# Reordering the head and the ticks of a DeltaNet and expert kernel

## The chip, the cores and the metric

The kernel runs on one core of a Trainium2 chip, as one program. The metric is the device time of one execution in microseconds. Its engines work on their own queues and in order: TensorE (PE, with its weight loads listed apart as PEld), VectorE (DVE), ScalarE (ACT), GpSimd (POOL) and SyncE (SP, which here only issues DMAs).

## The reference, cut to what matters

```
q, k, v: (4 batches, 8 heads, 768 positions, 48), beta: (4, 8, 768), float32
k_n = k / (norm(k) + 1e-6);  state = 0                      # state: 48 x 48 for each batch and head
for t in range(768):
    y[t]  = q[t] @ state
    state = state + beta[t] * outer(k_n[t], v[t] - k_n[t] @ state)
x = y of all heads side by side                             # 3072 tokens x 384
logits = x @ w_gate;  e = argmax(logits);  gate = softmax(logits)[e]
out = gate * (relu(x @ w1[e]) @ w2[e])                      # 8 experts, 384 -> 1024 -> 384
```

The recurrence is over positions. It is computed in blocks of 128 positions: with the products K K^T of a block known, the effect of the positions on each other is a triangular system, whose inverse turns residuals (v less what the state gives for k) into the updates u. Then y = q state + masked(Q K^T) u, and the state grows by K^T u.

## The kernel before, in words

There are NT = 6 blocks of 128 positions, B = 4 batches, so NN = 24 pieces n = 4 tb + b (block tb, batch b). Each block is split into four quarters of 32 positions. The order of all instructions is written out by hand (manual_schedule): a generator stands for a chain of work, and each `run` emits one step of it. Every engine executes what it is given in that order, so an instruction that waits holds up all that is behind it on its engine.

**Head.** Keys of the first four pieces are loaded, the diagonal 32 x 32 blocks of K K^T are made for block 0 (`kpart`, first step, "db") and inverse 0 runs on VectorE: `prepare(0)`, then `lanes(0)`, a forward substitution on 32 rows for 4 quarters and 32 batch-head pairs at once, in 32 steps of products (L332) and differences (L343) and 19 of the combination (L353, L361), then the turn into `wt` (L376). Beside it the other keys, v and q are loaded on SP, each load held back until a step of the inverse is done (`load`, `tiles["hold"]`). TensorE makes the full K K^T of eight pieces in the order `FILL` (`halves`, two PSUM banks of the pool "g", both evicted by ScalarE, L234); for blocks after 0 the diagonal blocks go to DRAM (`gd`, L239) and come back turned (`lg`, L243). Then come `dummy(W0)`, matmuls of 512 columns into a bank "x" with no use of their result, and `scale_v(0)`.

**Ticks.** The main loop has 27 ticks (t from 0 to 26). In tick t the first quarter of piece t, the second of t - 1, the third of t - 2 and the fourth of t - 3 are treated together, each on its 32 partitions. A tick emits, in this order:

- `residual(t)`: what state and earlier updates give for the keys, in PSUM "ks" (PE L403, L415); VectorE subtracts it from v (L422)
- `beside(t, 0)`: side work, see below
- `chunk(qs_, t)`: Q K^T of a piece (`qpart`, PE L252), eviction (ACT L262), mask on GpSimd (L263)
- `scale_v(t + 1)`: v times the key's norm (DVE L385); `clear_u`: a zero fill on GpSimd
- `beside(t, 1)`, then `dummy(WD.get(t, 0))`
- `apply(t)`: inverse times residual (PE L430), copied to u (ACT L434)
- `run(fin)`: the last part of the piece that was begun a tick earlier, x's turn (`emit_x`: PE L497, row copy ACT L498, reduction of the gate logits DVE L499); every so many pieces it starts `emit_slots` (a generator in `fine`), which finds each token's slot and scatters the rows (POOL L580)
- `beside(t, 2)`, and then the new `finish(t - 3)` in three steps: q times state (PE L449), state update (PE L459, ACT L463), masked Q K^T times u and y's copies (PE L469, ACT L473), with `beside` between them
- `chunk(ks_, t)`: K K^T of a later piece, `beside(t, 6)`, a zero fill of a DRAM region

`beside(t, i)` emits `STEPS[i]` steps (`STEPS0[i]` for t < 8) of the current inverse (`inverses`), up to three more of its `prepare`, `FINE[i]` steps of `emit_slots`, and at late ticks weight pieces and early expert work. Block tb's inverse has to be done before tick 4 tb; what is left then is emitted ahead of that tick.

**Slots.** `emit_slots` makes its counts on TensorE (L537, L540) into free columns of the bank "x" of the latest `emit_x`, and VectorE reads them (L544, L546 updates `base`).

**Expert phase.** From tick 20 on weights are loaded and split into high and low parts, and expert 0 begins; after tick 26 come the eight experts.

Of the kernel before, what the change touches and what calls it, by code (L numbers as in the profile page):

```python
# [42 lines left out]
def deltanet_moe(ctx, tc, qT, kT, kr, v, beta, w_gate, w1, w2, out):  # L43
# [62 lines left out]
    LAG = NB - 1  # L106
    FILL = (4, 5, 6, 0, 7, 1, 2, 3)

    STEPS = (3, 2, 3, 2, 2, 2, 2)

    STEPS0 = (3, 3, 3, 2, 2, 2, 2)
    FINE = (3, 3, 3, 2, 2, 2, 2)
    W0 = 18
    WD = {0: 10, 1: 6, 2: 6, 4: 6, 8: 6, 12: 6, 16: 6, 20: 6}
    W1 = 4
# [50 lines left out]
    tiles = {tb: {b: {} for b in range(B)} for tb in range(NT)}  # L166

    def load(out, in_):
        ins = nc.sync.dma_start(out=out, in_=in_)
        if "hold" in tiles:  # L170
            tc.add_manual_dep(ins.ins, tiles["hold"].name,
                              mybir.DependencyInfo(mybir.DependencyClass.Sync, mybir.DependencyReason.DATA),
                              reason="later loads wait")

# [34 lines left out]
    def kpart(n):  # L209
# [4 lines left out]
        if tb == 0:  # L214
# [16 lines left out]
            yield  # L231
        pg = halves(f"pg{tb}_{b}", kt, kt)
        for a in range(2):
# [11 lines left out]

    def halves(nm, kt, xt):

        pg = [psg_[-1].tile([128, NP, C], F32, name=f"{nm}_{a}", tag="g") for a in range(2)]
        for p in range(NP):
            for a in range(2):  # L250
                r = slice(64 * a, 64 * a + D)
                nc.tensor.matmul(pg[a][:, p], lhsT=kt[r, p], rhs=xt[r, p], start=True, stop=True,  # L252
                                 tile_position=(64 * a, 0), skip_group_check=True)
        return pg

    def qpart(n):

        tb, b = n // B, n % B
        pm = pm_t[n % QSL]
        pg = halves(f"pq{tb}_{b}", kt_t[n % KTL], qt_t[n % QTL])  # L260
        for a in range(2):
            nc.scalar.copy(out=pm[:, a:H:2], in_=pg[a])  # L262
        nc.gpsimd.affine_select(out=pm, in_=pm, compare_op=ALU.is_gt, fill=0.0, base=0,  # L263
                                pattern=[[0, H], [1, C]], channel_multiplier=-1)
        yield

    def clear_w(tb):
# [10 lines left out]
    def prepare(tb):  # L278
# [29 lines left out]
        yield  # L308
        def norms():
            for q in range(NB):  # L310
                p = slice(32 * q, 32 * q + 32)
                nc.vector.transpose(out=nt_t[p, (B * tb + q) * H:(B * tb + q) * H + 32], in_=s0[p])
                yield

# [7 lines left out]
    def lanes(tb):  # L322
# [23 lines left out]
        def combine(g):  # L346
# [11 lines left out]
            while n > 1:  # L358
                h, k = n // 2, n - n // 2
                y = x[:, :, 0:h] if n > 2 else lw[:, r0:r0 + 4, 0:HB].unsqueeze(2)  # L360
                nc.vector.tensor_tensor(out=y, in0=x[:, :, 0:h], in1=x[:, :, k:n], op=ALU.add)  # L361
                n = k
                yield
# [10 lines left out]
        yield  # L374
        T["wt"] = lp.tile([128, BH, 32], F32, name=f"wt{tb}", tag="wt", bufs=2)
        nc.vector.transpose(out=T["wt"].rearrange("p h t -> p t h"), in_=lw)  # L376
        if tb + 2 < NT:
# [46 lines left out]
    def apply(t):  # L424

        ks, vn = tiles["ks", t], vt[t]
        for h in range(H):
            for q, n in stage(t):
                r = slice(32 * q, 32 * q + 32)
                nc.tensor.matmul(ks[r, h, :], lhsT=tiles[n // B]["wt"][r, n % B * H + h, :], rhs=vn[r, h, :],  # L430
                                 start=True, stop=True, tile_position=(32 * q, 32 * q), skip_group_check=True)
# [6 lines left out]
    def finish(n):  # L438
# [41 lines left out]
        if j % m == 0:  # L480
            pool, tag = (fp, "rowb") if j >= 2 else (rp, "row") if n < NN - 2 else (xq_[0], "row")
            t = pool.tile([128, 2 if n < NN - 2 else 1, ROW], F32, name=f"row{tb}_{b}", tag=tag, bufs=2)
            tiles["rows"].append(t[:, 0:m])
        emit_x(n, yt, tiles["rows"][-1][:, j % m], tiles["rl"][:, j])
        if j == w - 1:
# [5 lines left out]

    def emit_x(n, yt, row, rl):

# [4 lines left out]
        nc.scalar.copy(out=row[:, 0:DM].rearrange("t (p c) -> t p c", p=NP), in_=xp[:, :, 0:2 * D])  # L498
        nc.vector.tensor_reduce(out=rl, in_=xp[:, :, 2 * D:].rearrange("t p e -> t e p"), axis=AX.X, op=ALU.add)  # L499

# [103 lines left out]
    def dummy(k):  # L604

        if k:
            wm = pss.tile([128, 512], F32, name=f"wm{next(cnt)}", tag="x")
        for _ in range(k):
# [221 lines left out]
    def more(n=1):  # L830
        for f, x in loads[:n]:
            tiles["hold"] = tiles["mark"]
            f(*((0, x) if f is load_v else (x,)))
# [68 lines left out]
    for t in range(NN + LAG):  # L902
        if t < NN and t % B == 0 and t > 0:
            while queue and queue[0][0] <= t // B:
                inverses(1, t)
            if t == NN - B:
# [3 lines left out]
                W = pieces()  # L910
                run(W)
        residual(t)
        if LAG <= t < NN - KTL + LAG:
            load_kt(t - LAG + KTL)
        beside(t, 0)
        chunk(qs_, t)
        if t + 1 < NN + LAG:
            scale_v(t + 1)
# [5 lines left out]
        run(copies, 2)  # L924
        run(fin)
        for tb in range(1, NT):
            for i in range(NB):
                if t == B * (tb - 1) + i:
                    load_v(tb, i)
        beside(t, 2)  # L930
        fin = finish(t - LAG) if t >= LAG else iter(())
        run(fin)
        beside(t, 3)
        run(fin)
        beside(t, 4)
# [288 lines left out]
```

## Time and profile before

| | |
|---|---|
| median of 3 runs | 578.01 us (576.63 to 578.91) |
| profiled execution | 578.77 us, its span 577.1 us |
| mean granted TensorE clock | 0.949 |
| PE busy | 507.3 us (88%) |
| DVE busy | 352.7 us (61%) |
| ACT busy | 254.8 us (44%) |
| POOL busy | 112.8 us (20%) |

The span begins at the first and ends at the last instruction; all times in the rows below count from its start. In the windows, the number of instructions stands behind each busy time, and the last two columns are the DMA engines' mean busy share and GB/s. Residual t begins at 42.20 us for t = 0, 75.06 for t = 4, 246.64 for t = 20 and 314.27 for t = 26. [...] A busy share is an average over stages that differ in what bounds them.

### The profile page before, as it was taken

The page shows a single profiled execution, that of the slowest core. Times are in us where ns is not written, and L with a number is a line of the kernel's source. Part 1 is how long each engine was busy: PE and PEld are TensorE (multiplying, and loading weights), DVE is VectorE, ACT ScalarE, POOL GpSimd, SP SyncE. Part 2 cuts the span into 40 slices and gives each one's busy share as a digit, 9 for nine tenths or more (in the row PEclk, how much of TensorE's full clock was granted, in tenths as well). Part 3 has the DMA queues.
Part 4 walks back from the last instruction along what each step waited for, and adds up shares of the span by engine and source line. Part 5 has one row for each costly group of instructions (what it writes and reads, how often), then busy time and mean ns, then how long its engine had stood idle before and what let it go on. Part 6 is the DMA issues. An engine that isn't in the chain of part 4 may idle for free.

```text
span 577.1 us, 17370 instructions
## 1 busy us (share of the span) xinstructions
PE 507.3 (88%) x7282; PEld 447.3 (78%) x7282; DVE 352.7 (61%) x1041; ACT 254.8 (44%) x536; POOL 112.8 (20%) x146
## 2 busy tenths in 40 slices
PE   3899599888878958788889899999999999999992
PEld 2767478767757836676678789999999999999992
DVE  2958959848858959844634229656475655655310
ACT  2323356545535724546634225445453635354310
POOL 5010212114113214313122111030203021211111
PEclk9999999879779979889989979999999999999997
DMA  3871576726615526264631254847474647563000
GB/s 108 242 195 38 165 225 181 186 92 171 182 43 194 134 61 198 92 204 153 206 106 44 71 118 156 191 153 182 133 161 143 171 145 163 154 150 98 26 17 24
DMA packets 77053, 79.00 MB, mean 137 GB/s; under 512 B 45721, under 2 KB 64714, under 8 KB 76972
## 3 DMA queue, kind: packets, MB, share of 16 engines
q1 hardware_dynamic: 73516, 68.29, 43.6%
q0 software_dynamic: 3456, 9.57, 4.5%
q8 instruction: 58, 0.95, 0.7%
q14 instruction: 23, 0.19, 0.1%
HBM read 54.25 MB, written 24.37 MB: 136 GB/s over the span
## 4 chain that ended last, share of the span: by engine, by line
PE 47%; DVE 8%; ACT 3%; issue 2%; DMA 2%; POOL 1%; SPq 0%; ACTq 0%; POOLq 0%; DVEq 0%
PE h L726 19%; PE y L736 16%; PE y L1018 4%; PE xp L497 1%; PE ks L430 1%; PE yp L469 1%; ACT u L434 1%; DVE lw L343 1%; DMA xr<-xg 1%; PE ks L403 1%; PE pq L252 1%; PE wm L609 1%; DVE ta L332 1%; ACT row L498 1%; PE ks L415 1%
## 5 line engine op out<-in xcount | busy, mean ns | idle before, releaser
L736 PE MATMUL y<-w2h,hx 128*128 128x384 f32 x352 | 92.8, 338 | 0.1
L739 POOL DMA_INDIRECT out_dram<-yo,idx x32 | 39.4, 1231 | 204.2 <-ACT yo L1013 116.7
L434 ACT COPY u<-ks 32x384 f32<-32x384 f32 x96 | 45.1, 469 | 51.9 <-PE ks L430 47.5
L736 PEld LDWEIGHTS y<-w2h,hx 128*128 128x128 f32 x352 | 64.0, 188 | 0.8 <-DVE hx L730 0.7
L726 PE MATMUL h<-xh,w1l 128*128 128x448 f32 x168 | 61.3, 365 | 0.0
L726 PE MATMUL h<-xl,w1h 128*128 128x448 f32 x168 | 61.2, 364 | 0.0
L726 PE MATMUL h<-xh,w1h 128*128 128x448 f32 x168 | 61.0, 363 | 0.0
L736 PE MATMUL y<-w2l,hx 128*128 128x384 f32 x176 | 59.3, 337 | 0.0
L730 DVE SCALAR_TENSOR_TENSOR hx<-h,hx 128x448 fp32r<-128x448 f32 (+1 forms) x64 | 37.6, 587 | 31.6 <-ACT hx L729 30.9
L616 DVE TENSOR_TENSOR w2l<-w2r,w2h 128x768 fp32r<-128x768 f32 x32 | 30.5, 957 | 42.3 <-ACT w2h L615 41.8
L729 ACT ACTIVATE hx<-h 128x448 fp32r<-128x448 f32 (+1 forms) x64 | 33.2, 519 | 49.6 <-PE h L726 46.2
L263 POOL TENSOR_SCALAR_AFFINE_SELECT pm<-pm 128x1024 f32<-128x1024 f32 x24 | 28.0, 1165 | 132.8 <-ACT pm L262 126.3
L403 PE MATMUL ks<-st,kt 112*32 112x96 f32 x768 | 45.9, 253 | 3.5 <-issue 3.0
L252 PE MATMUL pg<-kt 48*128 48x128 f32 x384 | 40.5, 342 | 8.3 <-DMA kt<-in_kT_dram 4.9
L262 ACT COPY pm<-pq 128x512 f32<-128x512 f32 x48 | 25.7, 588 | 45.8 <-PE pq L252 45.8
L252 PEld LDWEIGHTS pg<-kt 48*128 48x128 f32 x384 | 34.4, 236 | 14.1 <-issue 6.9
L430 PEld LDWEIGHTS ks<-v_all,wt 32*32 32x32 f32 x1536 | 22.1, 112 | 26.6 <-DVE v_all L422 20.6
L430 PE MATMUL ks<-v_all,wt 32*32 32x48 f32 x1536 | 26.0, 212 | 18.6 <-DVE v_all L422 18.0
L1013 ACT ACTIVATE yo<-y,gt 128x384 f32<-128x384 f32 x22 | 12.8, 581 | 63.7 <-PE y L736 36.3
L403 PEld LDWEIGHTS ks<-st,kt 112*32 112x32 f32 x768 | 33.6, 112 | 9.3 <-issue 5.0
L609 PE MATMUL wm<-zrow 128*128 128x512 bf16 x86 | 27.6, 476 | 14.9 <-DVE base L546 13.5
L499 DVE TENSOR_REDUCE rl<-xp 128x8 f32<-128x32 f32 x24 | 4.6, 191 | 53.7 <-ACT row L498 53.7
(161 smaller groups left out, 1103.5 us busy)
## 6 DMA issues: line engine op xcount, KB each, us to landing
w1r<-in_w_dram SPq DMA_DIRECT2D x24, 512.0 KB
w2r<-in_w_dram SPq DMA_DIRECT2D x32, 384.0 KB
xg<-zrow SPq DMA_DIRECT2D x7, 788.0 KB
kt<-in_kT_dram SPq DMA_DIRECT2D x24, 224.0 KB
qt<-in_qT_dram SPq DMA_DIRECT2D x24, 224.0 KB
xr<-xg SPq DMA_DIRECT2D x28, 168.0 KB
xn<-row SPq DMA_DIRECT2D x10, 394.0 KB
ku<-in_kr_dram SPq DMA_DIRECT2D x20, 192.0 KB
```

The source lines that it names most:

```text
L252: nc.tensor.matmul(pg[a][:, p], lhsT=kt[r, p], rhs=xt[r, p], start=True, stop=True, tile_position=(64 * a, 0), skip_group_check=True)
L263: nc.gpsimd.affine_select(out=pm, in_=pm, compare_op=ALU.is_gt, fill=0.0, base=0, pattern=[[0, H], [1, C]], channel_multiplier=-1)
L403: nc.tensor.matmul(ks[32 * q:32 * q + 32, 2 * p:2 * p + 2, :], lhsT=kt_t[n % KTL][0:RP, p, 32 * q:32 * q + 32], rhs=st_view(n % B, p), sta ...
L430: nc.tensor.matmul(ks[r, h, :], lhsT=tiles[n // B]["wt"][r, n % B * H + h, :], rhs=vn[r, h, :], start=True, stop=True, tile_position=(32 * ...
L434: nc.scalar.copy(out=uview(n)[r], in_=ks[r])
L609: nc.tensor.matmul(wm, lhsT=busy[:, 0:128], rhs=busy, start=True, stop=True)
L616: nc.vector.tensor_tensor(out=lo, in0=src, in1=hi.bitcast(F32), op=ALU.subtract)
L726: nc.tensor.matmul(ps, lhsT=w[:, d, fs], rhs=x_[:, d], start=(n == 0), stop=(n == len(terms) - 1))
L729: nc.scalar.activation(out=hh, in_=ps, func=AF.Relu)
L730: nc.vector.scalar_tensor_tensor(out=hl, in0=ps, scalar=0.0, in1=hh.bitcast(F32), op0=ALU.max, op1=ALU.subtract)
L736: nc.tensor.matmul(ps, lhsT=h(f)[h_], rhs=w2[w][:, f, :], start=(n == 0), stop=(n == len(terms) - 1))
L739: nc.gpsimd.indirect_dma_start(out=out, out_offset=bass.IndirectOffsetOnAxis(ap=idx, axis=0), in_=yo, in_offset=None, bounds_check=N - 1, ...
```

## The change

In the head: the order `FILL`, every second K K^T in the y banks, fewer dummies, written to a bank of y. In the ticks: x's turn of the earlier piece right after the residual and its reduction after `beside(t, 0)`; Q K^T after the first step of `finish`; the mask emitted just before the next residual, with a wait for the last step of the inverse before it (`after`, `tiles["mark"]`); 20 or 21 steps of the inverse in a tick; dummies in ticks 0 to 3 alone; v scaled four ticks at a time; v loaded one tick earlier. In the inverse: one transpose of the norms and four DMAs in place of four transposes, and a turn whose output is contiguous (`wt` is read with a step).

```diff
-    FILL = (4, 5, 6, 0, 7, 1, 2, 3)
-    STEPS = (3, 2, 3, 2, 2, 2, 2)
-    STEPS0 = (3, 3, 3, 2, 2, 2, 2)
+    FILL = (0, 1, 4, 5, 6, 7, 2, 3)
+    STEPS = (3, 3, 3, 3, 3, 3, 2)
+    STEPS0 = (3, 3, 3, 3, 3, 3, 3)
-    W0 = 18
-    WD = {0: 10, 1: 6, 2: 6, 4: 6, 8: 6, 12: 6, 16: 6, 20: 6}
+    W0 = 14
+    WD = {0: 6, 1: 6, 2: 6, 3: 3}
...
+    masks = []
+    def after(ins, why):
+        tc.add_manual_dep(ins.ins, tiles["mark"].name, ... Sync, ... DATA, reason=why)
...
-        pg = halves(f"pg{tb}_{b}", kt, kt)
+        pg = halves(f"pg{tb}_{b}", kt, kt, n in FILL[1::2])
...
-        pg = [psg_[-1].tile([128, NP, C], F32, name=f"{nm}_{a}", tag="g") for a in range(2)]
+        pg = [pss.tile([128, NP, C], F32, name=f"{nm}_{a}", tag=f"y{a}") if alt else
+              psg_[-1].tile([128, NP, C], F32, name=f"{nm}_{a}", tag="g") for a in range(2)]
...
-        nc.gpsimd.affine_select(out=pm, in_=pm, compare_op=ALU.is_gt, fill=0.0, base=0,
-                                pattern=[[0, H], [1, C]], channel_multiplier=-1)
-        yield
+        masks.append(pm)
+        yield
+
+    def mask():
+        while masks:
+            pm = masks.pop(0)
+            ins = nc.gpsimd.affine_select(out=pm, in_=pm, compare_op=ALU.is_gt, fill=0.0, base=0,
+                                          pattern=[[0, H], [1, C]], channel_multiplier=-1)
+            after(ins, "beside the residual")
...
         def norms():
+            sn = lp.tile([128, 32], F32, name=f"sn{tb}", tag="sn")
+            nc.vector.transpose(out=sn, in_=s0)
             for q in range(NB):
                 p = slice(32 * q, 32 * q + 32)
-                nc.vector.transpose(out=nt_t[p, (B * tb + q) * H:(B * tb + q) * H + 32], in_=s0[p])
-                yield
+                nc.sync.dma_start(out=nt_t[p, (B * tb + q) * H:(B * tb + q) * H + 32], in_=sn[p])
+            yield
...
-        T["wt"] = lp.tile([128, BH, 32], F32, name=f"wt{tb}", tag="wt", bufs=2)
-        nc.vector.transpose(out=T["wt"].rearrange("p h t -> p t h"), in_=lw)
+        T["wt"] = lp.tile([128, 32, BH], F32, name=f"wt{tb}", tag="wt", bufs=2)
+        tiles["mark"] = nc.vector.transpose(out=T["wt"], in_=lw).ins
...
     def scale_v(t):
+        if B <= t < NT * B:
+            if t % B == 0:
+                vn = v_t[:, t % VR:t % VR + B].rearrange("p t h d -> p (t h) d")
+                nc.vector.tensor_tensor(out=vn, in0=vn, in1=nt_t[:, t * H:(t + B) * H].unsqueeze(2)
+                                        .broadcast_to([128, BH, D]), op=ALU.mult)
+            return
...
-                nc.tensor.matmul(ks[r, h, :], lhsT=tiles[n // B]["wt"][r, n % B * H + h, :], rhs=vn[r, h, :],
+                nc.tensor.matmul(ks[r, h, :], lhsT=tiles[n // B]["wt"][r, :, n % B * H + h], rhs=vn[r, h, :],
...
-        emit_x(n, yt, tiles["rows"][-1][:, j % m], tiles["rl"][:, j])
+        xp = emit_x(n, yt, tiles["rows"][-1][:, j % m])
+        yield
+        nc.vector.tensor_reduce(out=tiles["rl"][:, j], in_=xp[:, :, 2 * D:].rearrange("t p e -> t e p"), axis=AX.X, op=ALU.add)
...
-            wm = pss.tile([128, 512], F32, name=f"wm{next(cnt)}", tag="x")
+            wm = pss.tile([128, 512], F32, name=f"wm{next(cnt)}", tag="y0")
...
+        mask()
         residual(t)
         if LAG <= t < NN - KTL + LAG:
             load_kt(t - LAG + KTL)
+        run(fin)
         beside(t, 0)
-        chunk(qs_, t)
-        if t + 1 < NN + LAG:
+        run(fin)
+        if t + 1 < NN + LAG and not B <= t + 1 < NN:
             scale_v(t + 1)
...
         run(copies, 2)
-        run(fin)
         for tb in range(1, NT):
             for i in range(NB):
-                if t == B * (tb - 1) + i:
+                if t == max(B * (tb - 1) + i - 1, 0):
                     load_v(tb, i)
         beside(t, 2)
         fin = finish(t - LAG) if t >= LAG else iter(())
         run(fin)
+        chunk(qs_, t)
         beside(t, 3)
...
         beside(t, 5)
+        if B <= t + 1 < NN:
+            scale_v(t + 1)
...
-    run(fin)
+    run(fin, 2)
```

`tiles["mark"]` is now also set by the combination's sums.

## Rows read from the trace of the kernel before

**Rows 1.** Windows of two stages: stretch, us, busy PE PEld DVE ACT POOL, clock, DMA.
```profile
75.06:246.64 171.58, 142.94 (x3695) 117.84 (x3693) 130.99 (x480) 87.19 (x216) 41.27 (x49) 0.90 0.50 144
246.64:314.27 67.63, 56.92 (x1263) 48.05 (x1261) 30.14 (x100) 34.58 (x81) 14.81 (x17) 0.95 0.46 146
```

**Rows 2.** Windows view by tick: ticks 4, 5, 7, 8, 11, 12 and 16.
```profile
75.06:85.62 10.56, 9.68 (x241) 7.49 (x239) 5.41 (x21) 5.79 (x14) 1.67 (x3) 1.00 0.61 192
85.62:93.34 7.72, 7.72 (x234) 6.81 (x233) 6.59 (x32) 5.57 (x13) 1.56 (x2) 1.00 0.65 222
102.18:113.47 11.29, 9.27 (x234) 8.05 (x232) 10.25 (x29) 5.67 (x13) 1.52 (x2) 0.85 0.69 170
113.47:128.49 15.02, 12.17 (x252) 9.18 (x250) 5.86 (x21) 6.18 (x18) 2.40 (x3) 0.77 0.27 79
147.14:159.87 12.73, 10.83 (x234) 9.37 (x233) 11.03 (x32) 5.87 (x13) 1.45 (x2) 0.73 0.62 180
159.87:176.16 16.29, 12.29 (x252) 9.24 (x250) 8.54 (x38) 6.27 (x18) 2.74 (x3) 0.79 0.17 50
201.80:217.82 16.02, 9.75 (x235) 6.96 (x233) 8.92 (x35) 5.01 (x17) 1.45 (x2) 0.79 0.23 60
```

**Rows 3.** Waits of the whole run: who, for whom, us in total, times, longest.
```profile
DVE rl L499 <- ACT row L498: 53.7, 21, 6.6
PE wm L609 <- DVE base L546: 13.5, 4, 6.2
```

**Rows 4.** Timeline of TensorE in tick 8: start, length, instructions, idle before.
```profile
119.50 2.74 PE L609 MATMUL wm<-zrow 128*128 128x512 bf16 x6 [2.85 <-DVE base L546]
122.17 1.50 PE L430 MATMUL ks<-v_all,wt 32*32 32x48 f32 x64
```

**Rows 5.** Timeline of tick 2: a mask on GpSimd, VectorE before and beside it.
```profile
57.99 0.20 DVE L332 TENSOR_TENSOR tb<-lg,lw 128x48 f32<-128x48 f32 x1
...
58.40 1.09 POOL L263 TENSOR_SCALAR_AFFINE_SELECT pm<-pm 128x1024 f32<-128x1024 f32 x1 [19.84 <-ACT pm L262]
58.43 1.11 DVE L343 TENSOR_TENSOR lw<-lw,tb 128x48 f32<-128x48 f32 x1
```

**Rows 6.** The subtract's line: ns shortest, median, longest; first and last start.
```profile
L422 DVE TENSOR_TENSOR v_all<-v_all,ks x28: 540/550/559, 43.1 to 315.8; 128x384 f32<-128x384 f32 x21, 32x384 f32<-32x384 f32 x3, 64x384 f32<-64x384 f32 x3, 96x384 f32<-96x384 f32 x1
```

**Rows 7.** Timeline of TensorE in the head: first K K^T, the dummies.
```profile
14.45 2.08 PE L252 MATMUL pg<-kt 48*128 48x128 f32 x16 [4.87 <-DMA kt<-in_kT_dram]
...
36.61 5.66 PE L609 MATMUL wm<-zrow 128*128 128x512 bf16 x18
```

**Rows 8.** Timeline of VectorE in the head: inverse 0 and what follows it.
```profile
10.11 1.25 DVE L283 STREAM_TRANSPOSE lg<-dg 128x1024 f32<-128x1024 f32 x1 [8.75 <-ACT dg L230]
...
14.81 0.20 DVE L332 TENSOR_TENSOR ta<-lg,lw 128x31 f32<-128x31 f32 x1
...
18.39 0.84 DVE L312 STREAM_TRANSPOSE nt_all<-s 32x32 f32<-32x32 f32 x4
...
28.39 2.23 DVE L353 TENSOR_TENSOR tc<-lw 128x512 f32<-128x512 f32 x4
...
34.89 1.95 DVE L376 STREAM_TRANSPOSE wt<-lw 128x1024 f32<-128x1024 f32 x1
43.09 0.54 DVE L422 TENSOR_TENSOR v_all<-v_all,ks 32x384 f32<-32x384 f32 x1 [6.25 <-PE ks L403]
43.56 0.17 DVE L288 TENSOR_SCALAR ss<-lg 128x32 f32<-128x32 f32 x1
```

**Rows 9.** Timeline of SP in the head: the read of block 1's diagonal.
```profile
35.87 0.34 SPq L243 DMA_DIRECT2D lg<-gd  x1
```

**Rows 10.** Weight loads of the apply, a strided and a contiguous line: ns shortest, median, longest.
```profile
L430 PEld LDWEIGHTS ks<-v_all,wt x1536: 101/105/166, 45.2 to 320.7; 32*32 32x32 f32 x192
L785 PEld LDWEIGHTS xt<-ident,xr x3: 189/196/210, 323.9 to 324.1; 128*128 128x128 f32 x3
L736 PEld LDWEIGHTS y<-w2h,hx x352: 186/188/192, 348.8 to 566.1; 128*128 128x128 f32 x176
```

More of the change, by code (lines that the diff above doesn't have):

```diff
@@ L166, in deltanet_moe @@
     tiles = {tb: {b: {} for b in range(B)} for tb in range(NT)}
+    masks = []
+    def after(ins, why):
+        tc.add_manual_dep(ins.ins, tiles["mark"].name,
+                          mybir.DependencyInfo(mybir.DependencyClass.Sync, mybir.DependencyReason.DATA), reason=why)
     def load(out, in_):
@@ L170, in load @@
         if "hold" in tiles:
-            tc.add_manual_dep(ins.ins, tiles["hold"].name,
-                              mybir.DependencyInfo(mybir.DependencyClass.Sync, mybir.DependencyReason.DATA),
-                              reason="later loads wait")
+            after(ins, "later loads wait")
     def load_kt(n):
@@ L244, in kpart, with halves @@
         yield
-    def halves(nm, kt, xt):
-        pg = [psg_[-1].tile([128, NP, C], F32, name=f"{nm}_{a}", tag="g") for a in range(2)]
+    def halves(nm, kt, xt, alt=False):
+        pg = [pss.tile([128, NP, C], F32, name=f"{nm}_{a}", tag=f"y{a}") if alt else
+              psg_[-1].tile([128, NP, C], F32, name=f"{nm}_{a}", tag="g") for a in range(2)]
         for p in range(NP):
@@ L360, in combine @@
                 y = x[:, :, 0:h] if n > 2 else lw[:, r0:r0 + 4, 0:HB].unsqueeze(2)
-                nc.vector.tensor_tensor(out=y, in0=x[:, :, 0:h], in1=x[:, :, k:n], op=ALU.add)
+                tiles["mark"] = nc.vector.tensor_tensor(out=y, in0=x[:, :, 0:h], in1=x[:, :, k:n], op=ALU.add).ins
                 n = k
@@ L490, in st_view, with emit_x @@
         return bass.AP(tensor=t.tensor, offset=t.offset, ap=[list(t.ap[0]), [64, 2], [1, D]])
-    def emit_x(n, yt, row, rl):
+    def emit_x(n, yt, row):
         tiles["bank"] = pss.tile([128, 512], F32, name=f"xp{n // B}_{n % B}", tag="x")
@@ L498, in emit_x @@
         nc.scalar.copy(out=row[:, 0:DM].rearrange("t (p c) -> t p c", p=NP), in_=xp[:, :, 0:2 * D])
-        nc.vector.tensor_reduce(out=rl, in_=xp[:, :, 2 * D:].rearrange("t p e -> t e p"), axis=AX.X, op=ALU.add)
+        return xp
     def emit_slots(tb, b, w, parts, rl):
@@ L831, in more @@
         for f, x in loads[:n]:
-            tiles["hold"] = tiles["mark"]
+            tiles["hold"] = True
             f(*((0, x) if f is load_v else (x,)))
```

## The prediction, made before the changed kernel ran

> **What bounds the kernel now.** I read the table by stages first. Ticks 4 to 19, in which the inverses of blocks 2 to 5 run beside the recurrence, take 171.6 us, 10.7 us each, and neither engine fills them: TensorE is busy 142.9, VectorE 131.0 [rows 1]. Ticks 20 to 25 take 67.6 us more; after tick 26 comes the expert phase, which the change does not touch.
>
> Next the table by ticks [rows 2]. Tick 5 is what TensorE needs: 7.72 us long, TensorE busy for all of it, clock 1.00. Tick 7 is what VectorE makes of it: 11.29 us, VectorE busy 10.25, clock 0.85. Ticks 4, 8, 12 and 16, the first of each group of four, take 10.56, 15.02, 16.29 and 16.02 us, though VectorE has only 5.4 to 8.9 us of work there.
>
> The waits say why [rows 3]. TensorE's dummy matmuls waited four times, 13.5 us, for VectorE's update of `base` (L546): they write the one "x" bank, which the slots' counts still occupy. In tick 8 the six dummies start after 2.85 us of that wait, run 2.74 us at the low clock, and the apply behind them takes 1.50 us [rows 4]. And VectorE waited 53.7 us, in 21 places, before the reduction of the gate logits (L499), which follows x's turn, which follows the apply; all inverse steps queued behind it wait too. So the ticks are bound by a ring: subtract, dummies, apply, x's turn, row copy, reduction, inverse steps, subtract.
>
> **The change part by part.** All sums are against the profiled execution, 578.77 us (span 577.07), which is 0.76 above the median of the runs.
>
> *Head.* VectorE ends inverse 0 with the turn at 34.89 + 1.95 = 36.84 and then waits 6.25 us until the first subtract at 43.09 [rows 8]: eighteen dummies run from 36.61 for 5.66 us [rows 7], behind eight K K^T products that started only at 14.45, when batch 4 had landed. Afterwards batches 0 and 1, already in SBUF, go first, and every second product uses the y banks, so that none waits for an eviction: six products of 2.08 us [rows 7] from 14.45 end near 27, and fourteen dummies at 5.66/18 = 0.31 us near 31.5. So VectorE comes last: 36.84, less 0.70 for the turn (1.95 against 1.25 for the one turn with a contiguous output, L283), less 0.63 for one transpose instead of four (0.84) [rows 8], is 35.5. The next operation, L288 (43.56), however needs block 1's diagonal from DRAM, whose read was issued at 35.87 [rows 9], behind eight writes that stand in SP's queue after the loads. That hardly moves. [...] Were VectorE's idle here filled by late key loads instead, the gain would be 3.
>
> *Ticks 0 to 3.* VectorE-bound. Two masks, moved beside the residual, give back 0.9 us each: the mask at 58.40 stretched an operation on 48 elements, 0.20 us long just before it, to 1.11 [rows 5], while the subtract, with one operand in PSUM, never took over 559 ns [rows 6]. That is -1.8; the transposes -0.6; apply(4) no longer behind six dummies -1.0. Against it, tick 2 ends in a TensorE wait of the kind after which the clock was low: +2.5 (priced below). Net **-0.9**.
>
> *Ticks 4 to 19.* I counted the steps as the program emits them: 17 for preparation (20 before), 51 products and sums, the flag, the turn. At 20 a tick they fall so: in the first tick preparation (11.36 to 14.81, 3.45 us) and 12 product steps (14.81 to 18.39, 3.58 us); in the second 20 product steps (19.23 to 28.39 less a scaling of 0.47: 8.7 us, 9.3 where it is 21); in the third 19 sums (28.39 to 34.89, 6.5 us); in the fourth only the turn, 1.25, and the grouped scaling [rows 8]. For blocks 4 and 5 preparation falls into the tick before and 20 product steps into the first (7.0 us). The scaling is 1536 elements; four products of 512 took 2.23 us, so 1.6 us, against four of 0.47 before: nothing gained. Subtract, reduction, slots and what a mask spills past the subtract add 1.1 to 1.6 us a tick. So VectorE needs about 8.6, 10.2, 7.5 and 5 us, TensorE 7.7 to 7.8 in each, and the larger counts: 8.6 + 10.2 + 7.8 + 7.8 = 34.4, in four groups about 138.
>
> That holds only if the rings are gone, and I think so: x's turn now stands between residual and apply, where Q K^T stood, and covers the subtract; its bank was read a tick earlier; the reduction follows the row copy without the apply's copies ahead of it. ScalarE has 5.6 us in 7.7 [rows 2], so the later Q K^T copies fit; if they did not, K K^T would wait under 1 us a tick. [...]
>
> In the second tick of each group TensorE still waits 10.2 - 7.7 = 2.5 us for the subtract. [...] Four times that: 138 + 9.3 = 147.7. Against 171.6: **-23.9**.
>
> *Ticks 20 to 26.* Six dummies go (0.31 each, 1.9 us), and the slots' chain starts before the apply. TensorE idles 67.63 - 56.92 = 10.7 us there [rows 1]. I take **-3** (bounds 0 and -7).
>
> *Weights at a step.* `wt` now keeps its 32 columns 128 bytes apart, and the apply loads them 1536 times at 105 ns [rows 10]. The transposes at L785 load 128 columns 12 bytes apart in 189 to 210 ns, contiguous ones (L736) in 186 to 192 [rows 10]. So a small step costs about 4%; 128 bytes is shown nowhere. I take 0, the value of the nearest row; the other end is below. [...]
>
> Sum: -5.5 - 0.9 - 23.9 - 3 = -33.3: 578.77 to 545.5, and 0.76 less for a median: **545 us**.
>
> **Rivals.**
> A. *The clock holds.* If waits are short or x's turn splits them, the low stretches (9.3 in the groups, 2.5 before) stay away: 545 - 11.8 = **533**. For it: over all sixteen ticks the clock averaged 0.90 [rows 1], so most waits cost none of it. Against: 2.5 us is longer than the waits of ticks 7 and 11.
> B. *Only the dummies' stall goes.* Ticks 4, 8, 12 and 16 took 57.9 us, the other twelve 113.7, or 9.48 each. If the four only come down to that, and uneven steps eat what masks and reductions give back, sixteen ticks take 151.6 (-20); with -4 for the head and nothing later, **554**. For it: 20 steps a tick crowd the first two ticks and leave the last empty. Against: the twelve contain mask stalls and waits at L499, which go.
> C. *The apply's loads.* Place: L430. At half clock its 64 loads and matmuls took 1.50 us [rows 4], 0.75 to 0.9 at full; 1536/64 is 24 such applies on the ring. Over 1.4 us more on each (about 2.6 times as long) the kernel is slower; at three times, 1.6 x 24 = 38, it takes **583**. For it: each column lies far from the next. Against: L785.
>
> **How the numbers follow.** Forecast 0.53 (its own range 538 to 551), A 0.25, B 0.17, C 0.05. The likeliest gives 545. The range takes in A, B and the bounds of head and late ticks: 529 to 561. A measurement of this kernel tells about 0.5%, 2.9 us, from no change. Faster by more: forecast, A and nearly all of B, 0.94; within: 0.02 from B and C; slower: most of C, 0.04.
>
> **What would show it.** Right: the first subtract near 36 and L288 near 38; no wait of a dummy for `base`; under 10 us of waits at L499 instead of 53.7; no two-operand SBUF product over 1 us in the ticks; ticks of about 8.6, 10.2, 7.8 and 7.8 us with one low-clock stretch per group; the turn at 1.25 us; L430's loads at 105 ns and the apply at 0.9 us. The steps fail if L288 stays beyond 41 (the transfer is the bound), if first ticks stay above 12 us, or if masks stretch products still. The whole is wrong if the sixteen ticks take over 160 us or the expert phase grows.

## The result, and the profile after

The changed kernel takes **571.32 us** (median of 20 runs, 563.97 to 577.70) where the kernel before takes 578.15 in the same comparison: ratio 0.9876, 95% interval 0.9849 to 0.9902. It is faster by 1.2%, some 7 us; 33 were forecast, and the time lies above the range. The profiled execution took 570.5 us, span 568.7, against 578.77 and 577.07. Some executions run over 1.5% longer than the fastest of the same kernel; most ratios below leave these out, but four of the six executions behind the last batch's 0.9622 are of that kind (mean granted clock 0.910 to 0.935, the other two 0.942 and 0.930).

By stage, in the profiled executions: up to residual 4, 75.06 us before and 74.53 after; ticks 4 to 19, 171.58 and 168.80; ticks 20 to 25, 67.63 and 64.29; from there to the end, 262.80 and 261.08. The sum of the differences, 0.5 + 2.8 + 3.3 + 1.7, is the 8.4 us between the spans. The stage from which 24 us should have come gave 3.

The windows view of the changed kernel answers [rows 1, 2]: ticks 4 to 19, ticks 20 to 25, then ticks 0, 2 and 3, then ticks 4, 8, 9, 11, 12 and 16.
```profile
74.53:243.33 168.80, 147.84 (x3672) 128.39 (x3670) 115.52 (x461) 87.44 (x217) 39.99 (x49) 0.86 0.55 153
243.33:307.62 64.29, 55.67 (x1256) 48.26 (x1254) 28.78 (x91) 34.68 (x81) 16.08 (x18) 0.97 0.48 152
...
27.47:42.69 15.22, 8.22 (x63) 6.47 (x62) 11.27 (x34) 1.84 (x5) 2.03 (x4) 0.74 0.55 135
...
50.16:65.23 15.07, 8.96 (x144) 7.37 (x143) 12.98 (x45) 3.86 (x8) 1.09 (x1) 0.78 0.59 165
65.23:74.53 9.30, 8.97 (x227) 7.65 (x227) 3.35 (x3) 4.70 (x12) 2.37 (x4) 0.81 0.42 109
...
74.53:88.84 14.31, 12.24 (x234) 10.42 (x233) 7.06 (x37) 6.08 (x15) 1.84 (x4) 0.66 0.73 210
117.49:130.71 13.22, 11.73 (x245) 10.17 (x244) 7.39 (x42) 6.38 (x19) 3.80 (x6) 0.74 0.51 152
130.71:141.10 10.39, 8.90 (x235) 7.45 (x233) 6.17 (x29) 5.49 (x13) 2.29 (x3) 1.00 0.73 231
149.79:157.77 7.98, 7.98 (x234) 7.08 (x232) 4.72 (x16) 5.57 (x14) 3.40 (x4) 1.00 0.53 154
157.77:172.81 15.04, 10.91 (x246) 9.52 (x244) 12.47 (x61) 6.30 (x19) 1.46 (x3) 0.77 0.51 138
200.91:215.05 14.14, 10.04 (x229) 8.60 (x228) 11.69 (x57) 6.11 (x19) 2.48 (x3) 0.78 0.42 132
```
Read the lengths against the forecast of 8.6, 10.2, 7.8 and 7.8. The first ticks of the four groups took 14.31, 13.22, 15.04 and 14.14, together 56.7 where 34.4 stood: 22.3 us too much, and the sixteen ticks as a whole came out 21.1 above the forecast 147.7. The other twelve took 112.1 where 113.3 stood, in sum about what they should, though not one by one. In ticks 12 and 16, together 12.0 us over, VectorE is busy 12.47 and 11.69 us. In ticks 4 and 8, together 10.3 over, it has 7 and TensorE is busy 12, at a granted clock (1.00 is full speed) of 0.66 and 0.74. TensorE's timeline of tick 4 has a stop in the middle of the residual that the profile gives no releaser for ("issue"), and the apply behind it takes 1.48 us at a clock of 0.55, about as long as that of [rows 4], 1.50 us at 0.50. Tick 8 has a stop of 0.93 us:
```profile
77.39 0.27 PE L422 MATMUL ks<-st,kt 112*32 112x96 f32 x1 [1.46 <-issue]
...
78.91 1.48 PE L449 MATMUL ks<-v_all,wt 32*32 32x48 f32 x64
```

The waits of the whole run (who, for whom, us in total, times, longest) answer [rows 3]:
```profile
DVE v_all L441 <- PE ks L434: 42.1, 13, 6.4
...
PE ks L449 <- DVE v_all L441: 24.6, 10, 5.9
...
DVE ss L299 <- DMA lg<-gd: 11.8, 3, 4.6
...
DVE rl L505 <- ACT row L519: 7.5, 10, 2.0
```
The reduction (now L505) waits 7.5 us instead of 53.7, and no dummy waits for `base` any more. Those waits are gone as forecast, and the time is not. What is left is the subtract (L441) waiting for the residual and the apply (L449) for the subtract, and a new row: block preparation (L299) waiting for its diagonal's read.

VectorE's timeline (start, length) shows the head, answering [rows 8, 9], and tick 12, whose residual starts at 157.77:
```profile
33.89 1.25 DVE L389 STREAM_TRANSPOSE wt<-lw 128x1024 f32<-128x1024 f32 x1
35.06 0.50 DVE L441 TENSOR_TENSOR v_all<-v_all,ks 32x384 f32<-32x384 f32 x1
38.88 0.19 DVE L299 TENSOR_SCALAR ss<-lg 128x32 f32<-128x32 f32 x1 [3.32 <-DMA lg<-gd]
...
154.49 0.19 DVE L554 TENSOR_TENSOR ohb<-oh,m_all 128x32 bf16<-128x32 f32 x1
159.28 0.19 DVE L299 TENSOR_SCALAR ss<-lg 128x32 f32<-128x32 f32 x1 [4.60 <-DMA lg<-gd]
...
161.09 1.70 DVE L399 TENSOR_TENSOR v_all<-v_all,nt_all 128x1536 f32<-128x1536 f32 x1
...
163.81 0.69 DVE L328 TENSOR_TENSOR lg<-lg,r 128x512 f32<-128x512 f32 x1
...
164.55 0.51 DVE L441 TENSOR_TENSOR v_all<-v_all,ks 128x384 f32<-128x384 f32 x1
```
In tick 12 VectorE has nothing from 154.7 on, since block 3's inverse is done; it waits 4.60 us for block 4's diagonal, then does the whole preparation and the grouped scaling, and only then the subtract, 6.8 us after the residual began. TensorE waits for it 3.53 us, and comes back at a clock of 0.50 (165.11 to 168.00 us):
```profile
161.20 0.39 PE L561 MATMUL xp<-ohb,ones 128*128 128x8 bf16 x10
165.11 1.51 PE L449 MATMUL ks<-v_all,wt 32*32 32x48 f32 x64 [3.53 <-DVE v_all L441]
```
The view of single lines (ns shortest, median, longest) answers [rows 5, 10] for the changed kernel:
```profile
L449 PEld LDWEIGHTS ks<-v_all,wt x1536: 126/146/166, 35.6 to 315.2; 32*32 32x32 f32 x192
L356 DVE TENSOR_TENSOR lw<-lw,ta x96: 211/355/845, 14.8 to 222.6; 128x31 f32<-128x31 f32 x6, 128x60 f32<-128x60 f32 x6, 128x87 f32<-128x87 f32 x6, 128x112 f32<-128x112 f32 x6
```
The apply's loads take 146 ns instead of 105, and the mask's stretching is nearly gone (845 ns at most on this line).

### The profile page after: what moved, and what is told of

It reads as the page before. It is cut to its first block, busy times and chain, and to the rows that moved or that the text cites. A ratio compares the mean times of both kernels' runs of the same rounds, so it can differ in the third digit from the quotient of the medians.

```text
span 568.7 us, 17324 instructions
## 1 busy us (share of the span) xinstructions
PE 508.0 (89%) x7242; PEld 458.7 (81%) x7247; DVE 332.3 (58%) x1008; ACT 254.7 (45%) x536; POOL 112.4 (20%) x146
## 4 chain that ended last, share of the span: by engine, by line
PE 72%; DVE 13%; issue 4%; DMA 4%; ACT 3%; SPq 2%; POOL 0%; ACTq 0%; DVEq 0%; POOLq 0%
PE h L747 21%; PE y L757 17%; PE pq L257 5%; PE ks L449 5%; PE y L1043 4%; PE yp L488 3%; DVE lw L356 3%; PE ks L422 3%; PE xp L518 3%; PE pg L257 2%; DVE ta L345 2%; PE yp L468 2%; PE sb L478 2%; PE ks L434 2%; SPq L243 1%
## 5 line engine op out<-in xcount | busy, mean ns | idle before, releaser
L449 PE MATMUL ks<-v_all,wt 32*32 32x48 f32 x1536 | 34.8, 228 | 30.1 <-DVE v_all L441 24.6
L449 PEld LDWEIGHTS ks<-v_all,wt 32*32 32x32 f32 x1536 | 30.1, 146 | 36.0 <-DVE v_all L441 27.8
L274 POOL TENSOR_SCALAR_AFFINE_SELECT pm<-pm 128x1024 f32<-128x1024 f32 x24 | 26.8, 1115 | 139.1 <-DVE lw L356 41.1
L422 PE MATMUL ks<-st,kt 112*32 112x96 f32 x768 | 47.3, 262 | 3.0 <-issue 3.0
L441 DVE TENSOR_TENSOR v_all<-v_all,ks 128x384 f32<-128x384 f32 (+3 forms) x28 | 15.3, 547 | 50.2 <-PE ks L434 42.1
L422 PEld LDWEIGHTS ks<-st,kt 112*32 112x32 f32 x768 | 35.1, 116 | 8.3 <-issue 5.8
L257 PE MATMUL pg<-kt 48*128 48x128 f32 x384 | 37.2, 347 | 3.1 <-ACT gg L238 2.2
L257 PEld LDWEIGHTS pg<-kt 48*128 48x128 f32 x384 | 32.9, 247 | 7.3 <-ACT gg L238 3.0
L637 DVE TENSOR_TENSOR w1l<-w1r,w1h 128x1024 fp32r<-128x1024 f32 x24 | 31.1, 1295 | 11.3 <-ACT w1h L636 10.3
L257 PE MATMUL pq<-qt,kt 48*128 48x128 f32 x384 | 36.9, 342 | 0.2 <-DVE xe L751 0.2
```

The source lines that it names most:

```text
L274: ins = nc.gpsimd.affine_select(out=pm, in_=pm, compare_op=ALU.is_gt, fill=0.0, base=0, pattern=[[0, H], [1, C]], channel_multiplier=-1)
L422: nc.tensor.matmul(ks[32 * q:32 * q + 32, 2 * p:2 * p + 2, :], lhsT=kt_t[n % KTL][0:RP, p, 32 * q:32 * q + 32], rhs=st_view(n % B, p), sta ...
L449: nc.tensor.matmul(ks[r, h, :], lhsT=tiles[n // B]["wt"][r, :, n % B * H + h], rhs=vn[r, h, :], start=True, stop=True, tile_position=(32 * ...
L637: nc.vector.tensor_tensor(out=lo, in0=src, in1=hi.bitcast(F32), op=ALU.subtract)
```

## The experiments

Each kernel stands against the kernel before on its own chip, in five rounds; kernels of one batch shared a chip. One caution first. The last batch ran the best version again: 0.9622 (0.9571 to 0.9673), where another chip had given **0.947** (0.9415 to 0.9526). Its two quickest executions, 545.82 and 550.54 us, are 0.946 and 0.954 of that batch's 577.15, so the spread of the executions explains most of the gap and the chips need not differ. Even so a difference of 1% between batches is not firm, and I compare kernels of one batch wherever there are such.

**Batch 1: four undoings in the changed kernel.**

*Contiguous weights.* Ratio 0.9867 (0.9813 to 0.992).
```
-  T["wt"] = lp.tile([128, 32, BH], ...);  transpose(out=T["wt"], in_=lw)
+  T["wt"] = lp.tile([128, BH, 32], ...);  transpose(out=T["wt"].rearrange("p h t -> p t h"), in_=lw)
```


> The changed kernel with wt laid out as before, so that the apply reads contiguous weights and the turn has a strided output again. Theory (the strided loads cost): an apply of 64 takes 1.13 us in the changed kernel against 0.88 before, and its loads 146 ns against 105; undone, 24 applies give back 0.25 us each, 6 us, less 0.7 for the first turn: about 566 against 571 us. Rival (the ticks are set by waits and by the clock, not by the apply): within 2 us of 571.


Its loads are back at 105 ns:
```profile
L449 PEld LDWEIGHTS ks<-v_all,wt x1536: 101/105/166, 35.4 to 308.5; 32*32 32x32 f32 x192
```
The time is not told apart from the changed kernel's 0.9876, which was measured outside this batch. The 6 us expected would be 1%, about what these intervals can part; the stride is not where the missing 26 us went.

*Preparation of blocks 4 and 5 a half tick later.* Ratio **0.9681** (0.9634 to 0.9728), 1.9% below its neighbour with contiguous weights, some 11 us.
```
-  READY = {..., 4: (3 * B - 1, 4), 5: (4 * B - 1, 4)}
+  READY = {..., 4: (3 * B, 0), 5: (4 * B, 0)}
```


> The changed kernel with preparation of blocks 4 and 5 held until ticks 12 and 16 begin. [...]


Its windows of ticks 12, 13 and 16:
```profile
155.08:164.04 8.96, 8.39 (x245) 7.42 (x244) 5.32 (x30) 6.06 (x19) 0.75 (x3) 1.00 0.66 176
164.04:178.88 14.84, 12.69 (x235) 10.35 (x233) 11.52 (x55) 5.83 (x14) 6.71 (x8) 0.77 0.59 190
193.68:201.50 7.82, 7.25 (x229) 6.40 (x227) 4.27 (x21) 5.02 (x18) 1.45 (x2) 1.00 0.55 149
```
Ticks 12 and 16 fall from 15.04 and 14.14 to 8.96 and 7.82, VectorE's work there from 12.47 to 5.32. A part comes back a tick later (tick 13: 14.84). The trace of a later kernel with the same edit and without dummies in these ticks (batch 3) has the same two lengths, 8.96 and 7.83.

*16 and 17 steps a tick instead of 20 and 21.* Ratio 0.9784 (0.9732 to 0.9836).
```
-  STEPS = (3, 3, 3, 3, 3, 3, 2);  STEPS0 = (3, 3, 3, 3, 3, 3, 3)
+  STEPS = (3, 2, 3, 2, 2, 2, 2);  STEPS0 = (3, 3, 3, 2, 2, 2, 2)
```


> The changed kernel with 16 inverse steps a tick (17 in the first eight) as before. [...] With 16 steps VectorE needs 7 to 8 us in every tick, as TensorE does: long waits go, 558 to 563 us. Rival (steps were not the cost): 571 within 3 us, low-clock stretches as long as before.


Some 0.8 to 1.0% better than its neighbours, at the edge of what the intervals part. Ticks 12 and 16 stay at 14.60 and 14.34 us: slower steps alone do not take the preparation out of them.

*Dummies again in ticks 4, 8, 12, 16 and 20.* Ratio 0.9888 (0.9844 to 0.9931).
```
-  WD = {0: 6, 1: 6, 2: 6, 3: 3}
+  WD = {0: 6, 1: 6, 2: 6, 3: 3, 4: 6, 8: 6, 12: 6, 16: 6, 20: 6}
```


> The changed kernel with six dummy matmuls again in ticks 4, 8, 12, 16 and 20 (in a y bank, so without the wait for base). Theory (waits and issue gaps set the low clock, dummies behind them do not): low stretches stay, dummies cost 1.3 to 2.7 us each time: 573 to 580 us. Rival (the missing dummies let the clock fall): the stretches after ticks 4, 8, 12 and 16 go, 560 us.


The clock of its sixteen ticks is 0.95 (this windows row) instead of 0.86, and they take 157.64 us instead of 168.80. But this profiled execution is the quickest of its six (561.55 us; the others 566.60 to 570.83), and the ratio does not differ. What the dummies' time and the higher clock are worth against each other is not settled here.
```profile
74.20:231.84 157.64, 141.16 (x3695) 120.52 (x3693) 116.33 (x461) 86.20 (x215) 38.82 (x48) 0.95 0.58 163
```

**Batch 2: the kernel before, with parts of the change; the head undone.**

*Only the dummies' bank.* Ratio **0.9823** (0.9777 to 0.9869): this one word is worth some 10 us, no less than the whole change.
```
-  wm = pss.tile([128, 512], F32, ..., tag="x")
+  wm = pss.tile([128, 512], F32, ..., tag="y0")
```


> The kernel before, only with its dummies in a y bank in place of the x bank. Theory of the prediction (the dummies' waits for base are a stall of their own): 13.5 us of waits in four ticks go, the apply no longer stands behind them: 565 to 568 against 578 us. Rival (the wait is that of x's turn for the same bank, right behind the apply, and passes to it): the waits reappear at L497, 575 to 578 us.


And its waits view still has the reduction's:
```profile
DVE rl L499 <- ACT row L498: 41.8, 22, 5.5
```

*That, and the new order of the tick.* Ratio 0.9844 (0.9791 to 0.9898).
```
-        emit_x(n, yt, row, rl)                     # turn and reduction behind the apply
+        xp = emit_x(n, yt, row);  yield            # turn behind the residual
+        nc.vector.tensor_reduce(out=tiles["rl"][:, j], ...)
-        chunk(qs_, t);  run(fin)
+        run(fin);  chunk(qs_, t)
```


> The same, and the order of the change alone: x's turn behind the residual, its reduction after the first side work, Q K^T after the first step of finish; steps, masks, head, weights, scaling as before. Theory (the reduction's 53.7 us of waits and the dummies' wait were the ring that bound the ticks): both go and, at 16 steps a tick with the dummies still there, the sixteen ticks take about 150 us in place of 171.6: 555 to 560 us. Rival (low clock and instruction supply set the ticks): 568 to 574 us.


The order adds nothing to the bank while the masks stay inline, though the reduction waits far less:
```profile
DVE rl L486 <- ACT row L500: 12.7, 10, 6.2
```
So most of the 53.7 us of waits at the reduction, which I put at the centre of the ring, cost no time. The subtract's waits for the residual rose from 14.0 to 27.1 us in their place.

*The head undone in the changed kernel.* Ratio 0.9989 (0.9954 to 1.0025).
```
-  FILL = (0, 1, 4, 5, 6, 7, 2, 3);  W0 = 14;  halves(..., n in FILL[1::2])
+  FILL = (4, 5, 6, 0, 7, 1, 2, 3);  W0 = 18;  halves(...)
```


> The changed kernel with the old order of the eight K K^T products, one pair of banks for all and 18 dummies. Theory (the head's 7 us reach the end): TensorE again holds the first subtract to about 43 us: 576 to 578 us against 571. Rival (ticks 0 to 3 swallow the head's gain, since residual 4 begins at 74.5 us against 75.1 before although the first subtract came 8 us sooner): within 3 us of 571.


VectorE's timeline of it has the old wait back (the first subtract at 42.02 instead of 35.06, the preparation of block 1 at 42.49 instead of 38.88), and without the head's edits next to nothing is left of the gain:
```profile
33.53 1.25 DVE L389 STREAM_TRANSPOSE wt<-lw 128x1024 f32<-128x1024 f32 x1
42.02 0.54 DVE L441 TENSOR_TENSOR v_all<-v_all,ks 32x384 f32<-32x384 f32 x1 [7.24 <-PE ks L422]
42.49 0.17 DVE L299 TENSOR_SCALAR ss<-lg 128x32 f32<-128x32 f32 x1
```

*Three undoings at once* (later preparation, 17 steps in ticks 0 to 7, dummies in 4, 8, 12, 16 and 20). Ratio 0.9607 (0.9549 to 0.9666).


> The changed kernel with three parts adjusted: preparation of blocks 4 and 5 held to ticks 12 and 16, 17 steps a tick in ticks 0 to 7, and six dummies in ticks 4, 8, 12, 16 and 20. Theory (the three losses are separate: 4 us in ticks 0 to 3, 8 us of waits for the diagonal, and low clock in the first ticks of a group): 552 to 556 us. Rival (one limit behind all three, supply of instructions or DMA): no better than the 557 us (ratio 0.968) of the held preparation alone.


The slow ticks are now 9, 13 and 17 (13.39, 13.82 and 12.41). In tick 9 TensorE waits in the apply for nothing that the profile shows, while GpSimd issues scatters, and then runs at a clock of 0.56 (122.00 to 129.04 us; in tick 13 at 0.50, 162.40 to 169.10):
```profile
117.53 0.99 POOL L601 DMA_INDIRECT xg<-row,sli  x1 [0.16 <-issue]
...
119.13 0.98 POOL L601 DMA_INDIRECT xg<-row,sli  x1 [0.16 <-issue]
...
119.78 0.26 PE L449 MATMUL ks<-v_all,wt 32*32 32x48 f32 x2 [0.29 <-issue]
...
120.41 0.97 POOL L601 DMA_INDIRECT xg<-row,sli  x1 [0.30 <-issue]
...
120.64 0.27 PE L449 MATMUL ks<-v_all,wt 32*32 32x48 f32 x2 [0.60 <-issue]
...
121.37 0.23 PE L449 MATMUL ks<-v_all,wt 32*32 32x48 f32 x1 [0.47 <-issue]
```

**Batch 3: variants of that kernel.**

*Masks inline again.* Ratio **0.9847** (0.9802 to 0.9892); its three neighbours have 0.9546 to 0.9583.
```
-  masks.append(pm)
+  nc.gpsimd.affine_select(out=pm, in_=pm, compare_op=ALU.is_gt, ...)
```


> The version with the three adjustments, but each mask emitted right behind its Q K^T again, without a wait for the inverse. Theory of the prediction (a mask stretches a product by about 0.9 us, on VectorE's path in about 10 of 24 places): 3 to 9 us slower, 557 to 563 us. Rival (VectorE is idle 1 to 4 us in most ticks by now, so the stretch is hidden): within 2 us of 554.


The neighbours differ from it in something more each (below), and none leads by less than 2.6%. In kernels with the new order the masks' new place is worth 2.6 to 3.0%, about 16 us; the masks' place without the new order was not tried.

*Without the copies of the row* (`xn<-row` left out). Ratio 0.9583 (0.9531 to 0.9634): the stops in ticks 9 and 13 stay (1.85 and 1.15 us; the ticks take 14.08 and 11.99), so these copies alone do not cause them.


> The version with the three adjustments, without the copies of all rows that serve only an expert with more than 448 tokens (they are left out; 10 writes, 394 KB each in the early ones). [...]

*Without the dummies of ticks 4, 8, 12, 16 and 20.* Ratio 0.9559 (0.9479 to 0.9639), its six executions between 547.52 and 559.30 us: not told apart from its neighbours that have them.


> The version with the three adjustments, less the dummies of ticks 4, 8, 12, 16 and 20. Theory (the dummies' 1.3 to 2.7 us each pay for themselves only if a low-clock stretch follows without them): 551 to 557, no clear difference. Rival (they hold the clock in the first ticks): first ticks of groups at a clock under 0.8 and 560 us or more.

*16 steps from tick 8 on as well, contiguous weights.* Ratio 0.9546 (0.949 to 0.9601): not told apart from the two above.


> The version with the three adjustments (0.961 of the kernel before), and besides 16 steps in all ticks and contiguous weights with the strided turn, as before the change. Theory (each is a small loss: 0.25 us on 24 applies, and ticks 5, 9, 13 crowded by 20 steps): 547 to 550 us, ratio 0.953. Rival (the preparation of blocks 4 and 5 at 16 steps no longer ends in its four ticks, so leftovers stand ahead of ticks 16 and 20): 556 us or more.

**Batch 4: what of the early preparation costs.**

*The diagonals of blocks 4 and 5 read a tick early*, steps in place. The read takes the diagonal of the block before, so this kernel leaves out the way of the new diagonal through DRAM and builds these two inverses from the older block, with as much work. Ratio 0.9862 (0.9814 to 0.9911).
```
-  if tb > 0 and b == B - 1:
+  if tb > 0 and b == (B - 2 if tb > 3 else B - 1):
-      dma_start(out=lg[:, 0:1024], in_=gd[tb])
+      dma_start(out=lg[:, 0:1024], in_=gd[tb - 1 if tb > 3 else tb])
```


> The changed kernel, steps and places as they are, but for blocks 4 and 5 the turned diagonal is read one tick earlier and from the block before (so these two inverses are of the wrong block; one read of the same size each): nothing waits for the way through DRAM. Theory (the wait of 4 to 5 us at ticks 11 and 15, and the low clock behind it, is the 11 us that holding the preparation gave): 560 to 563 us, ratio 0.970 to 0.975. Rival (it was the place of the 17 steps, which crowd ticks 11 and 12): 568 to 572, ratio 0.985 or more.


The wait for the read is gone from tick 12, and the tick still takes 13.71 us. VectorE's timeline there (residual at 150.69):
```profile
150.92 0.35 DVE L304 RECIPROCAL r<-s 128x32 f32<-128x32 f32 x1 [3.35 <-ACT s L302]
...
152.25 1.69 DVE L399 TENSOR_TENSOR v_all<-v_all,nt_all 128x1536 f32<-128x1536 f32 x1
...
155.71 0.51 DVE L441 TENSOR_TENSOR v_all<-v_all,ks 128x384 f32<-128x384 f32 x1
```
So it is not the transfer alone but the place: the preparation still stands in front of the subtract. It now waits for the square root on ScalarE, whose queue has its own order.

*17 steps in ticks 0 to 7 alone.* Ratio 0.9781 (0.9717 to 0.9844), 0.8% below the neighbour above.
```
-  STEPS0 = (3, 3, 3, 3, 3, 3, 3)
+  STEPS0 = (3, 3, 3, 2, 2, 2, 2)
```


> The changed kernel with 17 steps a tick in ticks 0 to 7 alone, 20 later. Theory (ticks 0 to 2 are bound by VectorE and with 21 steps tick 3 is left with nothing but TensorE's work): residual 4 begins near 70 instead of 74.5 us, 566 to 567 us. Rival: the later low-clock stretches shift and swallow it, within 2 us of 571.


As much as 16 and 17 steps everywhere gave on another chip (0.9784), so the later ticks' 20 steps cost nothing that shows. Residual 4 starts at 69.37 in its trace, and at 74.53 in the changed kernel: 5.2 us.

*The best version*: later preparation, 16 and 17 steps, contiguous weights. **539.46 us**, ratio **0.947** (0.9415 to 0.9526).


> The changed kernel with preparation of blocks 4 and 5 held, 16 and 17 steps a tick, contiguous weights, and no dummies from tick 4 on. Theory (dummies after tick 4 cost about what they save): 547 to 550 us, ratio 0.952. Rival (at 16 steps the dummies do hold the clock): 553 us or more.


Its sixteen ticks take 148.16 us. That this is near the forecast's 147.7 is chance: this is another kernel, and its first ticks took 13.19, 11.94, 10.24 and 8.33 us, not 8.6.
```profile
68.88:217.04 148.16, 134.10 (x3671) 115.96 (x3669) 117.92 (x457) 86.68 (x215) 41.62 (x48) 0.92 0.62 172
```

*The kernel before with the bank, the order and the masks.* **544.8 us**, ratio **0.9601** (0.9545 to 0.9657).
```
-  nc.gpsimd.affine_select(out=pm, ...)            # beside the inverse steps
+  masks.append(pm)                                # emitted with a dependency on the last step
```


> The kernel before with the dummies in a y bank, the order of the change (0.984 so far) and its masks beside the residual, all else as before. Theory (a mask stretches a product by 0.9 us and VectorE is the bound in two ticks of three): 553 to 558 us, ratio 0.960 to 0.967. Rival (the masks cost only where steps are crowded): 565 to 568.


Old head, old step counts, old weights and scaling, and 2.6% faster than the changed kernel with early reads on the same chip. Its sixteen ticks take 142.45 us at a clock of 0.98:
```profile
77.00:219.45 142.45, 130.26 (x3692) 110.80 (x3694) 126.89 (x485) 86.57 (x216) 40.12 (x47) 0.98 0.62 176
```
The sums of a pair of products with the masks inline (the kernel of batch 2 with the new order), and with them beside the residual:
```profile
L343 DVE TENSOR_TENSOR lw<-lw,ta x96: 211/358/1298, 14.8 to 219.0; 128x31 f32<-128x31 f32 x6, 128x60 f32<-128x60 f32 x6, 128x87 f32<-128x87 f32 x6, 128x112 f32<-128x112 f32 x6
```
```profile
L353 DVE TENSOR_TENSOR lw<-lw,ta x96: 211/362/762, 14.6 to 204.4; 128x31 f32<-128x31 f32 x6, 128x60 f32<-128x60 f32 x6, 128x87 f32<-128x87 f32 x6, 128x112 f32<-128x112 f32 x6
```
The longest falls from 1298 to 762 ns.

**Batch 5: the weights once more, where TensorE bounds more of the ticks.** The best version again, 0.9622 (0.9571 to 0.9673), and the same with the strided weights, 0.9586 (0.9543 to 0.9629). By these ratios no difference shows, but the first kernel's executions spread from 545.82 to 557.88 us and the second's from 551.25 to 555.08, so the 6 us in question stay open.


> The best version once more (preparation of blocks 4 and 5 a half tick later, 16 and 17 steps a tick, contiguous weights), to stand beside the next kernel on one chip: 0.947 of the kernel before, within 0.006.

> The best version with the strided weights of the change put back (and the turn at 1.25 us). Theory: where TensorE sets the pace, 0.25 us on each of 24 applies reaches the end: 6 us, 0.010 of the kernel before, less 0.7 us for each turn on VectorE's path: ratio 0.955 to 0.957. Rival (it is hidden in the waits for VectorE, as it was when the contiguous weights were put into the changed kernel itself): within 0.003 of the best version.

## Why the prediction was wrong

The step that failed is the term "Ticks 4 to 19: -23.9", which measured -2.8: the sixteen ticks took 168.80 us, past the 160 at which the forecast called itself wrong, and first ticks stayed above 12 us. (Its sum had a slip too: 138 and 9.3 are 147.3, not 147.7.) What failed in it first is the sentence that for blocks 4 and 5 "preparation falls into the tick before and 20 product steps into the first (7.0 us)". Preparation is let loose by `READY` near the end of the group's last tick, and I charged it to that tick, which has room. In the trace it waits there for the diagonal's read (4.60 us) and so runs in the first tick after all, together with the product steps: 12.47 us of VectorE's work where I had 7.0 and the subtract. And it runs in front of the subtract, for which TensorE waits; what stands behind a waiting instruction on its engine I had not asked here. Ticks 12 and 16 together came out 12.0 us over the forecast, and moving that one placement gave 1.9%, 11 us. Reading the diagonal early gave nothing clear (0.9862, on another chip) while the steps stayed in front of the subtract, and neither did slower steps clear the two ticks. The same `READY` did little harm in the kernel before with bank, order and masks (ticks 12 and 16: 10.0 and 9.5 us). There the read is waited for 0.98 us, the scalings come in four pieces, and the subtract starts 4.0 us after the residual; in the changed kernel 6.8, with slower steps 5.9, with the early read 5.0. Which of the grouped scaling, the later read and the faster steps makes the difference was not tried one by one.

The other 10.3 us over the forecast, in ticks 4 and 8, are not the preparation's: `READY` puts that of blocks 2 and 3 behind the subtract, which started 3.46 and 1.81 us after the residual. I had put the low clock into the second tick of a group, behind a wait for the subtract; here it fell in the first, after TensorE had stopped 1.46 and 0.93 us for nothing that the profile shows. No run settles what stopped it.

Point by point:

- *Head -5.5*: right. The first subtract came at 35.06 (forecast 36), the turn took 1.25. The term ran to the preparation of block 1, which came at 38.88 (forecast 38) against 43.56: -4.7. No run shows the 2 us that I assumed for the read's landing; in this trace the read was issued at 35.70, and VectorE waited for it 3.32 us, until 38.88. With the head undone the ratio is 0.9989 against 0.9876, from two batches, and this preparation comes 3.6 us later than in the changed kernel.
- *Ticks 0 to 3, -0.9*: wrong. From the preparation of block 1 to residual 4 it was 31.5 us before (43.56 to 75.06) and is 35.7 (38.88 to 74.53): +4.2. With the head undone it is 35.6, and with seventeen steps 31.0 (38.36 to 69.37), close to the 30.6 forecast, so it is the steps that cost this. Twenty-one steps crowd ticks 0 and 2 (VectorE 11.27 and 12.98 us busy) and leave tick 3 with 3.35. Seventeen steps give 0.8 to 1.0% back. I counted the steps of ticks 4 to 19 one by one, and not these.
- *Masks*: right in kind, but priced only in part. I gave 0.9 us to each of two masks in ticks 0 to 3; in the later ticks their worth stood inside the -23.9 without a figure of its own. 24 masks are worth about 16 us, 0.7 for each on average, where one stretched operation loses 0.9.
- *Dummies' bank*: right, some 10 us by itself. That is rival B's first half, without the rest.
- *The ring through the reduction*: over-read. The waits fell from 53.7 to 7.5 us, and the order, tried with the bank alone, is worth nothing.
- *Low clock, 9.3*: too small for this kernel. No run shows one stretch of 2.3 us a group: that, like the 2.5 us taken for tick 2, was my estimate from TensorE's busy time in ticks 7 and 11 [rows 2], where the clock was 0.50 from 108.20 to 111.60 us and 0.51 from 152.50 to 159.40. The changed kernel's clock was 0.86 over sixteen ticks: 0.77 and 0.78 in ticks 12 and 16, where the waits are longer, and 0.66 and 0.74 in ticks 4 and 8, where TensorE stopped. Whether dummies would pay for the clock measured with them (0.95) is not settled. Rival A (the clock holds) describes the kernel before with bank, order and masks: 0.98.
- *Weights at a step, 0*: the loads take 146 ns, not 105. In the bare tick TensorE needs 7.98 instead of 7.72 us, 0.26 for each apply; 24 of them would be 6 us on the path, which neither of the two comparisons shows or rules out. L785, which I took as the nearest row, has a step of 12 bytes and shows little of the effect (196 ns against 188 at the median, [rows 10]). Rival C's threshold of 1.4 us was far off.
- *Ticks 20 to 26, -3*: right, -3.3. *Grouped scaling, nothing gained*: right, 1.70 us.

So much of the size that I forecast is there, in part by luck: the order of the tick, which I put at the centre, added nothing, and the masks were not priced by themselves where they gave most. The bank (1.8%) and the masks (2.6% or more) are some 25 us, the head some 5. The preparation's place took 11 back and the crowded first ticks 5. That would leave a gain of 14 us where 7 were measured. These worths come from different batches and from kernels with different neighbours, so such a sum can be off by several us; the stops of TensorE fall into the rest, and I leave it open.

## What to carry to other kernels

Where work is released by its position, follow what it waits for there and what is queued behind it on its engine: a preparation with room in its tick came to stand, with its wait, ahead of the one instruction that another engine needs. A long wait in the list is worth what its engine's being late costs, so try the smallest piece of a change by itself: here one bank's name gave as much as the whole. The best kernel measured keeps the bank, the masks and the head of this change, and the old step counts with later preparation; the old step counts and placement with the new head and masks alone were not tried.

## What the runs showed of the hardware

A GpSimd mask (1.09 us in [rows 5]) stretched a VectorE operation with both inputs in SBUF to about its own length (1.11 us there; at most 1298 ns on the line of sums above, with the masks inline). The subtract, with one operand in PSUM, stayed as it was: 4 of the 28 subtracts ran beside a mask in the kernel before, 6 in the changed kernel, none over 559 ns, and 12 in the kernel before with bank, order and masks, none over 558. Moving 24 masks was worth 2.6 to 3.0%. The apply's weight load of 32 columns 128 bytes apart took 146 ns at the median, with the columns side by side 105. TensorE had idle stretches of 0.3 to 1.7 us with nothing that the profile shows to wait for: 13 us of them in the first 300 us of the changed kernel, 6 before. In tick 9 above they came while scatters and loads kept the DMA engines at a share of 0.88, and a clock of 0.56 followed (0.95 in this row):
```profile
115.65:122.00 6.35, 4.99 (x156) 4.14 (x155) 5.30 (x26) 1.61 (x4) 4.53 (x5) 0.95 0.88 292
```
What stops it there stays open; leaving out the row copies did not end it.
